# A decode step with its gradients: the scores of both halves of a chunk summed in one array tile and brought back by one-pass transposes, q and out_0 computed as rows

## The chip, the cores and the metric

One NeuronCore of one Trainium2 chip. The metric is the device time of one execution in microseconds (us). Every comparison uses runs that were rated fast, taken in alternation with the kernel before on the same chip.

## The reference, cut to what matters

A decode step of attention with 32 heads and a cache of 8192 positions, a gated MLP beside it, and the gradients of both. The gradients of the K and V caches (`out_2`, `out_3`) are as large as the caches. So all of K and V is read, and as much is written: four times 67 MB, 268 of the kernel's 303.5 MB.

```python
B, Sq, D = 1, 1, 640
Hq, Hkv, Sk, Dh = 32, 32, 8192, 128                    # bfloat16
xn = _layernorm(x)
q = (xn @ wq).reshape(B, Sq, Hq, Dh).transpose(0, 2, 1, 3)
scores = jnp.einsum("bhqd,bhkd->bhqk", q, k) * (Dh ** -0.5)
p = _softmax(scores, axis=-1)
o = jnp.einsum("bhqk,bhkd->bhqd", p, v)                # then @ wo
# + x + (silu(x @ w1) * (x @ w3)) @ w2
# reference(): the output and its vjp for x, k_cache, v_cache, wq, wo, w1, w3, w2
```

## The kernel before

For each head, K and then V (128 partitions of 64 rows of 128 bf16) go through TensorE: sixteen chunks are transposed as pairs of bf16 in fp32 words (`T`), multiplied by q or by the output gradient (`Mp`), the scores are evicted (`ev`) and brought back to one row a position by selection matmuls (`selm`). Then come softmax, the weighted sums over V and K (`wsum`), the outer products on VectorE, which overwrite K and V by their gradients, and the stores. Below are the parts that the change or the argument touches; `...` marks cuts, set-up lines of the functions are left out, and the line numbers are those of the profile.

```python
def prep_q(g, ps, first):                                # once for each group of four heads
    for hh in range(GH):
        for ci in range(NC):                             # 20 loads and matmuls of one column, L260
            nc.tensor.matmul(ps[:, hh:hh + 1], lhsT=G_["wq"][:, ci, hh * DH:(hh + 1) * DH],
                             rhs=xn_col_bf[:, ci:ci + 1], ...)
    nc.scalar.activation(G_["cb"][:, 0, :], ps, ACTF.Copy, scale=scale)

def T(h, kind, c):                                       # L305, L307
    pT = pst()
    for k in range(4):
        nc.tensor.transpose(pT[:, k * P:(k + 1) * P], W3[:, 4 * c + k, :], ident_f[:])
    KT = kt_tile()                                       # one of four buffers
    nc.scalar.copy(KT[:].rearrange("p k w -> p (k w)"), pT[:])

def Mp(h, kind, c0):                                     # QW = 32: four column groups, L324
    for c in (c0, c0 + 1):
        KTb = ...
        for par in range(2):
            q = QW * (2 * (c - c0) + par)
            o = QL + QW * (2 * a + par) - c0
            nc.tensor.matmul(S_[kind][q:q + QW, :], lhsT=S_["qz"][:, o:o + QW], rhs=KTb[:, par, :], ...)

def ev(h, kind):                                         # L330
    XS = kt_tile()
    nc.scalar.copy(XS[:].rearrange("p k w -> p (k w)"), S_.pop(kind)[:])

def selm(h, kind):                                       # L340: four fp32 matmuls, two passes each
    for k in range(4):
        nc.tensor.matmul(S_["m"][:, b0:b0 + J].rearrange("p (c k t) -> p k c t", k=4, t=2)[:, k, :, :],
                         lhsT=XS[:, k, :], rhs=selc[:].rearrange("p (c t) -> p c t", t=2), ...)

def store(kind, h):
    t = kv_tiles.pop((kind, h))
    fifo((dkc if kind == "K" else dvc)[h], t[:])
    free_slots.append(t)
    load_next()                                          # the next K or V goes into this buffer

# the end of a head's order of work
Mp(h, "V", NCH - 2)
ev(h, "V")
o_sum(h)                 # 16 matmuls of 512 columns: all that PE has during the eviction
selm(h, "V")
rdot(h)
...
# fin_pe: out_0, once for each group: 20 loads and matmuls of one column
for hh in range(GH):
    for ci in range(NC):
        nc.tensor.matmul(acc[:, OUT0 + ci:OUT0 + ci + 1], lhsT=G_["wo"][:, hh, ci * P:(ci + 1) * P],
                         rhs=G_["od_bf"][:, hh, 0:1], ...)
```

## Time and profile before

| | before |
|---|---|
| time, median of 3 runs | 732.5 us (732.12 to 733.51) |
| span of the profiled run | 730.6 us, mean granted TensorE clock 0.881 |
| TensorE busy | 606.6 us (83%), 5669 matmuls |
| DMA share, 20 to 690 us | 1.01 (424 to 428 GB/s from 100 us on) |
| PE's waits for K and V, 280 to 690 us | 30.8 us |

How to read it: a DMA share of 1.01 means that all 16 DMA engines are busy all the time. A granted clock of 0.88 means that TensorE did not run at full speed all the time. PE in a profile line is TensorE, PEld its loads of weights, DVE VectorE and ACT ScalarE; `L340` is a line of the kernel. The groups of instructions that the change touches were these (busy us, mean ns of one, idle time before and what ended it):

```profile
L340 PE MATMUL m<-selc,KT 128*128 128x16 f32 x512 | 73.2, 276 | 22.7 <-ACT KT L330 22.5
L324 PE MATMUL sA<-KT,qz 128*32 128x512 bf16 x512 | 55.1, 421 | 0.0
L330 ACT COPY KT<-dA 128x512 f32<-128x512 f32 x32 | 19.3, 604 | 0.6 <-PE dA L324 0.6
```

The selection matmuls (L340) wait 22.5 us for the eviction of the scores (L330), and each of these fp32 matmuls counts twice (x512 for 256 in the program).

### The profile page before, as it was taken

Reading aid. Unit: us, or ns where it says so; the run is one execution under the profiler, and the core shown is the slowest. Engines: PE = TensorE matmul, PEld = TensorE weight load, DVE = VectorE, ACT = ScalarE, POOL = GpSimd, SP = SyncE. Lnnn points to the kernel's source line nnn. Section 1 sums busy time; section 2 is a strip of 40 time slices with the busy share of each in tenths; the row PEclk is TensorE's granted clock in tenths of the full one; section 3 lists DMA queues with packets and bytes.
Section 4 is the critical chain, followed back from the end, with each engine's and each line's share of the span. In section 5 each row is a group of like instructions: output and inputs, shape, how many; then the busy total and the mean of one; then the engine's idle time right before and its main releaser. Section 6 shows DMA issues by size and latency. Waiting matters only on the chain.

```text
span 730.6 us, 13869 instructions
## 1 busy us (share of the span) xinstructions
PE 606.6 (83%) x5669; PEld 423.1 (58%) x5669; DVE 459.3 (63%) x806; ACT 369.4 (51%) x719; POOL 29.9 (4%) x45
## 2 busy tenths in 40 slices
PE   3989589998899889988987887888898889978940
PEld 2657466666566656666655555566566556655620
DVE  4069646677757776776646765547756756667482
ACT  2650736656556556554655554545554536655510
POOL 0010110000100000001000000000000000000000
PEclk9996699999999999988998998979897969989765
DMA  9999999999999999999999999999999999999993
GB/s 354 400 411 420 425 421 432 415 429 425 417 416 426 429 427 421 430 428 426 425 428 426 431 423 427 429 428 428 427 424 429 429 427 428 428 434 426 425 393 155
DMA packets 27145, 303.58 MB, mean 416 GB/s; under 512 B 2807, under 2 KB 4153, under 8 KB 10441
## 3 DMA queue, kind: packets, MB, share of 16 engines
q1 hardware_dynamic: 21328, 276.39, 89.5%
q0 software_dynamic: 5728, 26.30, 8.9%
q8 instruction: 44, 0.72, 0.4%
q14 instruction: 21, 0.16, 0.1%
q10 hardware_dynamic: 24, 0.01, 0.0%
HBM read 151.34 MB, written 151.34 MB: 414 GB/s over the span
## 4 chain that ended last, share of the span: by engine, by line
PE 42%; DMA 41%; DVE 8%; ACT 6%; issue 1%; SPq 0%; ACTq 0%; DVEq 0%
DMA out_dram<-kv 22%; PE pT L305 20%; DMA kv<-in_A_k_cache_dram 11%; DMA kv<-in_A_v_cache_dram 7%; PE m L340 6%; PE X L417 5%; ACT KT L307 4%; PE sA L324 4%; DVE kv L450 3%; PE dA L324 2%; DMA wo_g<-in_A_wo_dram 2%; DVE side L251 1%; PE gu_ps L527 1%; ACT KT L330 1%; PE m L430 1%
## 5 line engine op out<-in xcount | busy, mean ns | idle before, releaser
L307 ACT COPY KT<-pT 128x512 f32<-128x512 f32 x512 | 289.5, 589 | 235.3 <-PE pT L305 200.6
L305 PE MATMUL pT<-ident_f,kv 128*128 128x128 f32 x2048 | 318.7, 296 | 40.6 <-DMA kv<-in_A_k_cache_dram 17.9
L305 PEld LDWEIGHTS pT<-ident_f,kv 128*128 128x128 f32 x2048 | 248.5, 154 | 97.0 <-PE pT L305 27.8
L450 DVE TENSOR_TENSOR kv<-qd,U 128x4096 bf16<-128x4096 bf16 x64 | 146.0, 2284 | 0.0
L450 DVE TENSOR_TENSOR kv<-qd,P 128x4096 bf16<-128x4096 bf16 x64 | 143.6, 2284 | 0.0
L340 PEld LDWEIGHTS m<-selc,KT 128*128 128x128 f32 x512 | 67.4, 205 | 45.8 <-ACT KT L330 34.1
L340 PE MATMUL m<-selc,KT 128*128 128x16 f32 x512 | 73.2, 276 | 22.7 <-ACT KT L330 22.5
L417 PE MATMUL X<-kv,Z 128*32 128x512 bf16 x1024 | 85.3, 462 | 1.8 <-DVE Z L434 1.8
L400 DVE SCALAR_TENSOR_TENSOR U<-m,P 128x64 bf16<-128x64 f32 x32 | 7.4, 233 | 104.9 <-PE m L340 104.9
L324 PE MATMUL dA<-KT,qz 128*32 128x512 bf16 x512 | 55.2, 418 | 0.2 <-ACT KT L307 0.2
L324 PE MATMUL sA<-KT,qz 128*32 128x512 bf16 x512 | 55.1, 421 | 0.0
L324 PEld LDWEIGHTS <-qz 128*32 128x32 bf16 x1024 | 26.6, 93 | 42.8 <-issue 41.6
L417 PEld LDWEIGHTS <-Z 128*32 128x32 bf16 x1024 | 28.6, 110 | 33.9 <-issue 16.6
L366 DVE TENSOR_REDUCE mrow<-m 128x1 f32<-128x64 f32 x32 | 7.1, 223 | 62.9 <-PE m L340 62.9
L360 ACT CAST qd<-pT 128x256 bf16<-128x256 f32 x32 | 11.9, 372 | 48.6 <-DVE kv L450 32.4
L500 DVE SCALAR_TENSOR_TENSOR wq_g<-wq_g,side 128x512 bf16<-128x512 bf16 x40 | 27.3, 683 | 0.0
L251 DVE SCALAR_TENSOR_TENSOR side<-wo_g,g_bc 128x640 bf16<-128x640 bf16 x32 | 26.2, 819 | 1.1 <-DMA wo_g<-in_A_wo_dram 0.8
L373 DVE TENSOR_REDUCE negM<-m 128x1 f32<-128x128 f32 x32 | 9.3, 291 | 24.5 <-PE m L370 24.5
L432 DVE SCALAR_TENSOR_TENSOR U<-m,P 128x128 bf16<-128x128 f32 x32 | 11.4, 355 | 18.0 <-PE m L430 18.0
L390 DVE RECIPROCAL rZ<-m 128x1 f32<-128x1 f32 x32 | 5.3, 167 | 24.1 <-PE m L384 24.1
L330 ACT COPY KT<-dA 128x512 f32<-128x512 f32 x32 | 19.3, 604 | 0.6 <-PE dA L324 0.6
L330 ACT COPY KT<-sA 128x512 f32<-128x512 f32 x32 | 19.3, 603 | 0.0
(154 smaller groups left out, 365.2 us busy)
## 6 DMA issues: line engine op xcount, KB each, us to landing
out_dram<-kv SPq DMA_DIRECT2D x64, 2048.0 KB, 31.1
kv<-in_A_k_cache_dram SPq DMA_DIRECT2D x32, 2048.0 KB, 25.2
kv<-in_A_v_cache_dram SPq DMA_DIRECT2D x32, 2048.0 KB, 26.3
out_dram<-wo_g POOLq DMA_DIRECT2D x8, 640.0 KB, 11.4
out_dram<-wq_g POOLq DMA_DIRECT2D x8, 640.0 KB, 12.9
wq_g<-in_A_wq_dram POOLq DMA_DIRECT2D x7, 640.0 KB, 13.2
wo_g<-in_A_wo_dram POOLq DMA_DIRECT2D x7, 640.0 KB, 19.3
kv<-in_B_w_dram SPq DMA_DIRECT2D x2, 1728.0 KB, 28.7
```

The lines of the kernel that those rows point to most:

```text
L251: nc.vector.scalar_tensor_tensor(junk[:], G_["wo"][:, hh, :], 1.0, g_bc[:], ALU.mult, ALU.mult, accum_out=G_["do"][:, hh:hh + 1])
L305: nc.tensor.transpose(pT[:, k * P:(k + 1) * P], W3[:, 4 * c + k, :], ident_f[:])
L307: nc.scalar.copy(KT[:].rearrange("p k w -> p (k w)"), pT[:])
L324: nc.tensor.matmul(S_[kind][q:q + QW, :], lhsT=S_["qz"][:, o:o + QW], rhs=KTb[:, par, :], start=(c0 == 0), stop=(c0 == NCH - 2), skip_grou ...
L330: nc.scalar.copy(XS[:].rearrange("p k w -> p (k w)"), S_.pop(kind)[:])
L340: nc.tensor.matmul(S_["m"][:, b0:b0 + J].rearrange("p (c k t) -> p k c t", k=4, t=2)[:, k, :, :], lhsT=XS[:, k, :], rhs=selc[:].rearrange( ...
L360: nc.scalar.copy(qd[:].rearrange("p a d -> p (a d)"), hd[h].pop("ps_r"))
L373: nc.vector.tensor_reduce(S_["negM"][:], S_["m"][:, 2 * J:2 * J + P], AX.X, ALU.max, negate=True)
L417: nc.tensor.matmul(xg["X"][q:q + QW, :], lhsT=Z[:, o:o + QW], rhs=W[:, N4 * i:N4 * (i + 1)], start=(slot == 0 and i < 4), stop=(slot == NS ...
L432: nc.vector.scalar_tensor_tensor(S_["U2"][:], S_["V"][:, 0:J].unsqueeze(2).to_broadcast([P, J, 2]), S_["m"][:, OC + NS:OC + NS + 1], S_["P ...
L450: nc.vector.tensor_tensor(dst[:, lo * DH:hi * DH].rearrange("p (j a b) -> p j a b", a=DH // 2, b=2), vec.rearrange("p (a b) -> p a b", b=2 ...
L500: nc.vector.scalar_tensor_tensor(wq_g[:, ci, :], wq_g[:, ci, :], 1.0, dqb, ALU.mult, ALU.mult, accum_out=dxa[:, ci, g:g + 1])
```

## The change

The intent is less work on TensorE. The two halves (`par`) of a chunk are summed in the same array tile, in two rounds, so the scores take 64 partitions instead of 128. A sum of halves by the selection matrix is then no longer needed, and the way back is a permutation: a transpose, which needs one pass instead of two (the transposes of L305 count once, x2048 for 2048 in the program, the matmuls of L340 twice). q and out_0 become rows, with the weights as moving operand: few long matmuls instead of many loads of weights. The core of the diff:

```diff
+    def out_row(vec, mat):
+        k = mat.shape[0]
+        for e in range(2):
+            nc.tensor.matmul(acc[64 * e:64 * (e + 1), 0:DHALF], lhsT=vec.to_broadcast([k, 64]),
+                             rhs=mat[:, e * DHALF:(e + 1) * DHALF], start=False, stop=True, skip_group_check=True)
...
+    def prep_q(g):
+        pq = pst()
+        for ci in range(NC):
+            nc.tensor.matmul(pq[:], lhsT=xn_col_bf[:, ci:ci + 1].to_broadcast([P, P]), rhs=G_["wq"][:, ci, :], ...)
+        G_["qrow"] = t_tile()
+        nc.scalar.activation(G_["qrow"][0:1, 0:GW], pq[0:1, :], ACTF.Copy, scale=scale)
+    def prep_qc(g, ps, first):
+        for hh in range(GH):
+            nc.tensor.matmul(ps[:, hh:hh + 1], lhsT=qrow[0:1, hh * DH:(hh + 1) * DH], rhs=one_bf[0:1, :], ...)
...
     def Mp(h, kind, c0):
-            for par in range(2):
-                q = QW * (2 * (c - c0) + par)
+        for par in range(2):
+            for c in (c0, c0 + 1):
+                q = QW * (c - c0)
                 o = QL + QW * (2 * a + par) - c0
...
     def ev(h, kind):
-        nc.scalar.copy(XS[:].rearrange("p k w -> p (k w)"), S_.pop(kind)[:])
+        nc.scalar.copy(XS[0:QH].rearrange("p k w -> p (k w)"), S_.pop(kind)[0:QH, :])      # QH = 64
...
     def selm(h, kind):
         for k in range(4):
-            nc.tensor.matmul(S_["m"][:, b0:b0 + J].rearrange("p (c k t) -> p k c t", k=4, t=2)[:, k, :, :],
-                             lhsT=XS[:, k, :], rhs=selc[:].rearrange("p (c t) -> p c t", t=2),
-                             start=(kind == "K" and k == 0), stop=True, skip_group_check=True)
+            nc.tensor.matmul(S_["m"][:, b0:b0 + 4 * J].rearrange("p (x c k t) -> p k x c t", x=4, k=4, t=2)[:, k],
+                             lhsT=XS[0:QH, k, :], rhs=selc[0:QH].rearrange("p (x c t) -> p x c t", x=4, t=2),
+                             start=(kind == "K" and k == 0), stop=True, is_transpose=True, skip_group_check=True)
...
     # fin_pe, and likewise in the MLP
-            for ci in range(NC):
-                nc.tensor.matmul(acc[:, OUT0 + ci:OUT0 + ci + 1], lhsT=G_["wo"][:, hh, ci * P:(ci + 1) * P], ...)
+            out_row(G_["od_bf"][:, hh, 0:1], G_["wo"][:, hh, :])
```

Cut: small MLP tiles move into a buffer that is free by then, the sum for the gradient of x moves to another bank and is reduced earlier, x is added to out_0 by matmul, and out_0 is stored from a row, ahead of `out_1`.

More of the change, by code (lines that the diff above doesn't have):

```diff
@@ L193 @@
     RX = 64
-    dx_acc = acc[:, 0:NC * RX].rearrange("p (c r) -> p c r", r=RX)
-    OUT0 = NC * RX
+    DHALF = D // 2
+    def out_row(vec, mat):
[3 more added lines that the diff above has]
+                             rhs=mat[:, e * DHALF:(e + 1) * DHALF], start=False, stop=True, skip_group_check=True)
     negmean = consts.tile([P, 1], F32, name="negmean")
@@ L254, in prep_do @@
             nc.vector.tensor_copy(G_["cb"][:, 1, :], G_["do"][:])
-    def prep_q(g, ps, first):
+    def prep_q(g):
         G_ = grp[g]
-        for hh in range(GH):
-            for ci in range(NC):
-                nc.tensor.matmul(ps[:, hh:hh + 1], lhsT=G_["wq"][:, ci, hh * DH:(hh + 1) * DH],
-                                 rhs=xn_col_bf[:, ci:ci + 1], start=(first and hh == 0 and ci == 0),
-                                 stop=(ci == NC - 1), skip_group_check=True)
-        nc.scalar.activation(G_["cb"][:, 0, :], ps, ACTF.Copy, scale=scale)
+        pq = pst()
+        for ci in range(NC):
+            nc.tensor.matmul(pq[:], lhsT=xn_col_bf[:, ci:ci + 1].to_broadcast([P, P]), rhs=G_["wq"][:, ci, :],
+                             start=(ci == 0), stop=(ci == NC - 1))
+        G_["qrow"] = t_tile()
+        nc.scalar.activation(G_["qrow"][0:1, 0:GW], pq[0:1, :], ACTF.Copy, scale=scale)
+    def prep_qc(g, ps, first):
+        G_ = grp[g]
+        qrow = G_.pop("qrow")
+        for hh in range(GH):
+            nc.tensor.matmul(ps[:, hh:hh + 1], lhsT=qrow[0:1, hh * DH:(hh + 1) * DH], rhs=one_bf[0:1, :],
+                             start=(first and hh == 0), stop=True, skip_group_check=True)
+        nc.scalar.copy(G_["cb"][:, 0, :], ps)
     def prep_sel(g, ps):
@@ L289 @@
     Z_vals = Z[:, QW - 4:].rearrange("p (i n) -> p i n", n=QW)[:, :, 0:4]
-    selc = consts.tile([P, 2 * NCH], F32, name="selc")
-    nc.vector.tensor_tensor(
-        selc[:].rearrange("p (e o t) -> p o e t", o=2, t=2),
-        ident_f[:].rearrange("p (o b n) -> p o b n", b=2, n=QW)[:, :, 0, 0:NCH].rearrange(
-            "p o (e t) -> p o e t", t=2),
-        ident_f[:].rearrange("p (o b n) -> p o b n", b=2, n=QW)[:, :, 1, 0:NCH].rearrange(
-            "p o (e t) -> p o e t", t=2), ALU.add)
+    QH = 2 * QW
+    selc = consts.tile([P, QH], F32, name="selc")
+    for x in range(QW // NCH):
+        nc.vector.tensor_copy(
+            selc[:, 2 * NCH * x:2 * NCH * (x + 1)].rearrange("p (e o t) -> p o e t", o=2, t=2),
+            ident_f[:, 0:QH].rearrange("p (o x e t) -> p x o e t", o=2, e=NCH // 2, t=2)[:, x])
     def new_head(h):
@@ L317, in Mp @@
                 S_["V"] = ps_d.tile([P, 512], F32, name="dA", tag="dA")
+        KTb = {}
         for c in (c0, c0 + 1):
-            KTb = S_["kt"].pop((kind, c))[:].rearrange("p k w -> p (k w)").bitcast(BF16).rearrange(
+            KTb[c] = S_["kt"].pop((kind, c))[:].rearrange("p k w -> p (k w)").bitcast(BF16).rearrange(
                 "p (n two) -> p two n", two=2)
-            for par in range(2):
-                q = QW * (2 * (c - c0) + par)
+        for par in range(2):
+            for c in (c0, c0 + 1):
+                q = QW * (c - c0)
                 o = QL + QW * (2 * a + par) - c0
-                nc.tensor.matmul(S_[kind][q:q + QW, :], lhsT=S_["qz"][:, o:o + QW], rhs=KTb[:, par, :],
-                                 start=(c0 == 0), stop=(c0 == NCH - 2), skip_group_check=True)
+                nc.tensor.matmul(S_[kind][q:q + QW, :], lhsT=S_["qz"][:, o:o + QW], rhs=KTb[c][:, par, :],
+                                 start=(c0 == 0 and par == 0), stop=(c0 == NCH - 2 and par == 1),
+                                 skip_group_check=True)
     def ev(h, kind):
@@ L486, in fin_pe @@
         for hh in range(GH):
-            for ci in range(NC):
-                nc.tensor.matmul(acc[:, OUT0 + ci:OUT0 + ci + 1], lhsT=G_["wo"][:, hh, ci * P:(ci + 1) * P],
-                                 rhs=G_["od_bf"][:, hh, 0:1], start=False, stop=True, skip_group_check=True)
+            out_row(G_["od_bf"][:, hh, 0:1], G_["wo"][:, hh, :])
     def fin_wo(g):
@@ L519, with mt @@
     blocks_f = [(b, min(P, F - b * P)) for b in range(NB)]
-    hcol = consts.tile([P, NB], F32, name="hcol")
+    mt_f = mA[:, NA * F:].bitcast(F32)
+    mt_at = [0]
+    def mt(cols):
+        r = mt_f[:, mt_at[0]:mt_at[0] + cols]
+        mt_at[0] += cols
+        return r
+    hcol = mt(NB)
     def mlp():
@@ L546, in mlp @@
                                  start=False, stop=True, skip_group_check=True)
-        gu = consts.tile([P, 2, NB], F32, name="gu")
-        nc.vector.memset(gu[:], 0.0)
+        gu = mt(2 * NB).rearrange("p (w b) -> p w b", w=2)
+        nc.vector.memset(gu, 0.0)
         nc.vector.tensor_copy(gu[:, :, 0:NFULL], gu_ps[:, :, 0:NFULL])
@@ L553, in mlp @@
         up = gu[:, 1, :]
-        dhc = consts.tile([P, NB], F32, name="dhc")
-        nc.vector.tensor_reduce(dhc[:], dh_ps[:], AX.X, ALU.add)
-        sig = consts.tile([P, NB], F32, name="sig")
-        nc.scalar.activation(sig[:], gate, ACTF.Tanh, scale=0.5)
-        nc.vector.tensor_scalar(sig[:], sig[:], 0.5, 0.5, ALU.mult, ALU.add)
-        silu = consts.tile([P, NB], F32, name="silu")
-        nc.vector.tensor_tensor(silu[:], gate, sig[:], ALU.mult)
-        nc.vector.tensor_tensor(hcol[:], silu[:], up, ALU.mult)
@@ L562, in mlp @@
-        hcol_bf = consts.tile([P, NB], BF16, name="hcol_bf")
-        nc.vector.tensor_copy(hcol_bf[:], hcol[:])
-        dgu = consts.tile([P, 2, NB], F32, name="dgu")
-        nc.vector.tensor_tensor(dgu[:, 1, :], dhc[:], silu[:], ALU.mult)
-        t1 = consts.tile([P, NB], F32, name="t1")
-        nc.vector.tensor_scalar(t1[:], sig[:], -1.0, 1.0, ALU.mult, ALU.add)
-        nc.vector.tensor_tensor(t1[:], t1[:], gate, ALU.mult)
-        nc.vector.tensor_scalar(t1[:], t1[:], 1.0, None, ALU.add)
@@ L570, in mlp @@
-        nc.vector.tensor_tensor(t1[:], t1[:], sig[:], ALU.mult)
-        nc.vector.tensor_tensor(dgu[:, 0, :], dhc[:], up, ALU.mult)
-        nc.vector.tensor_tensor(dgu[:, 0, :], dgu[:, 0, :], t1[:], ALU.mult)
-        dgu_bf = consts.tile([P, 2, NB], BF16, name="dgu_bf")
-        nc.vector.tensor_copy(dgu_bf[:], dgu[:])
+        dhc = mt(NB)
+        nc.vector.tensor_reduce(dhc, dh_ps[:], AX.X, ALU.add)
+        sig = mt(NB)
+        nc.scalar.activation(sig, gate, ACTF.Tanh, scale=0.5)
+        nc.vector.tensor_scalar(sig, sig, 0.5, 0.5, ALU.mult, ALU.add)
@@ new lines, in mlp @@
+        silu = mt(NB)
+        nc.vector.tensor_tensor(silu, gate, sig, ALU.mult)
+        nc.vector.tensor_tensor(hcol, silu, up, ALU.mult)
+        hcol_bf = mt(NB // 2).bitcast(BF16)
+        nc.vector.tensor_copy(hcol_bf, hcol)
+        dgu = mt(2 * NB).rearrange("p (w b) -> p w b", w=2)
+        nc.vector.tensor_tensor(dgu[:, 1, :], dhc, silu, ALU.mult)
+        t1 = mt(NB)
+        nc.vector.tensor_scalar(t1, sig, -1.0, 1.0, ALU.mult, ALU.add)
+        nc.vector.tensor_tensor(t1, t1, gate, ALU.mult)
@@ L575, in mlp @@
+        nc.vector.tensor_scalar(t1, t1, 1.0, None, ALU.add)
+        nc.vector.tensor_tensor(t1, t1, sig, ALU.mult)
+        nc.vector.tensor_tensor(dgu[:, 0, :], dhc, up, ALU.mult)
+        nc.vector.tensor_tensor(dgu[:, 0, :], dgu[:, 0, :], t1, ALU.mult)
+        dgu_bf = mt(NB).bitcast(BF16).rearrange("p (w b) -> p w b", w=2)
+        nc.vector.tensor_copy(dgu_bf, dgu)
         for b, rows in blocks_f:
             wsrc = w2a[:, b, :] if b < NBA else w2b[:, b - NBA, :]
-            for ci in range(NC):
-                nc.tensor.matmul(acc[:, OUT0 + ci:OUT0 + ci + 1], lhsT=wsrc[0:rows, ci * P:(ci + 1) * P],
-                                 rhs=hcol_bf[0:rows, b:b + 1], start=False, stop=True, skip_group_check=True)
+            out_row(hcol_bf[0:rows, b:b + 1], wsrc[0:rows, :])
@@ new lines, in mlp @@
+        x_cb = mt(4).bitcast(BF16)[:, 0:NC]
+        nc.vector.tensor_copy(x_cb, x_col[:])
+        for ci in range(NC):
+            for e in range(2):
+                lo, hi = max(ci * P, e * DHALF), min((ci + 1) * P, (e + 1) * DHALF)
+                if lo < hi:
+                    nc.tensor.matmul(acc[64 * e:64 * (e + 1), lo - e * DHALF:hi - e * DHALF],
+                                     lhsT=x_cb[:, ci:ci + 1].to_broadcast([P, 64]),
+                                     rhs=ident_bf[:, lo - ci * P:hi - ci * P], start=False, stop=True,
+                                     skip_group_check=True)
@@ L605, in mlp @@
                 nc.scalar.copy(bc_sb[:, wi, f0:f1], pb[:, 0:f1 - f0])
+        dx_acc = ps_d.tile([P, NC, RX], F32, name="dx_acc", tag="dA")
+        nc.vector.memset(dx_acc[:], 0.0)
         FA, FB = 256, 832
@@ L633, in mlp @@
         load_next()
+        nc.vector.tensor_reduce(dxm[:], dx_acc[:], AX.X, ALU.add)
+    dxm = consts.tile([P, NC], F32, name="dxm")
     gate = consts.tile([P, 1], F32, name="gate")
@@ L674, in side_pe1, with side_pe1b @@
         elif hh == 3 and g + 1 < NG:
-            prep_q(g + 1, hd[h]["m"][:, 320:320 + GH], False)
+            prep_q(g + 1)
+    def side_pe1b(h):
+        g, hh = divmod(h, GH)
+        if hh == 3 and g + 1 < NG:
+            prep_qc(g + 1, hd[h]["m"][:, 320:320 + GH], False)
     def side_pe2(h):
@@ L732, in head @@
         T(h, "V", 7)
+        side_pe1b(h)
         Mp(h, "V", 4)
@@ L762 @@
     ps_0 = pst()
-    prep_q(0, ps_0[:, 0:GH], True)
+    prep_q(0)
+    prep_qc(0, ps_0[:, 0:GH], True)
     for hh in range(GH):
@@ L786 @@
         fin_wq(NG - 1, ci)
-    fin = consts.tile([P, 2 * NC], F32, name="fin")
-    dxm = consts.tile([P, NC], F32, name="dxm")
-    nc.vector.tensor_reduce(dxm[:], dx_acc, AX.X, ALU.add)
+    fin = consts.tile([P, NC], F32, name="fin")
     dxn = consts.tile([P, NC], F32, name="dxn")
@@ L793 @@
     nc.vector.tensor_tensor(dxn[:], dxn[:], dxm[:], ALU.add)
-    nc.vector.tensor_tensor(fin[:, 0:NC], acc[:, OUT0:OUT0 + NC], x_col[:], ALU.add)
+    row_bf = t_tile()[:, 0:DHALF]
+    nc.vector.tensor_copy(row_bf, acc[:, 0:DHALF])
+    out_0v = out_0.rearrange("a b (e c) -> (a b e) c", e=2)
+    for e in range(2):
+        nc.scalar.dma_start(out_0v[e:e + 1, :], row_bf[64 * e:64 * e + 1, :])
     st = consts.tile([P, 2], F32, name="st")
@@ L805 @@
     nc.vector.tensor_scalar(t5[:], t5[:], nst[:, 0:1], rstd[:], ALU.add, ALU.mult)
-    nc.vector.tensor_tensor(fin[:, NC:2 * NC], t5[:], g_col[:], ALU.add)
+    nc.vector.tensor_tensor(fin[:], t5[:], g_col[:], ALU.add)
     ps_o = pst()
-    nc.tensor.transpose(ps_o[0:2 * NC, 0:P], fin[:], ident_f[:])
-    fin_bf = consts.tile([2 * NC, P], BF16, name="fin_bf")
-    nc.vector.tensor_copy(fin_bf[:], ps_o[0:2 * NC, 0:P])
-    for dst, r0, cuts in ((out_0, 0, (0, 3, 5)), (out_1, NC, (0, 4, 5))):
-        for lo, hi in zip(cuts, cuts[1:]):
-            nc.scalar.dma_start(dst.rearrange("a b (c p) -> (a b c) p", p=P)[lo:hi, :], fin_bf[r0 + lo:r0 + hi, :])
+    nc.tensor.transpose(ps_o[0:NC, 0:P], fin[:], ident_f[:])
+    fin_bf = consts.tile([NC, P], BF16, name="fin_bf")
+    nc.vector.tensor_copy(fin_bf[:], ps_o[0:NC, 0:P])
+    nc.scalar.dma_start(out_1.rearrange("a b (c p) -> (a b c) p", p=P), fin_bf[:])
 _INS = ['A_x', 'A_k_cache', 'A_v_cache', 'A_wq', 'A_wo', 'B_x', 'B_w1', 'B_w3', 'B_w2', 'grad_out']
```

## The prediction

> **What bounds the kernel now.** I began with the page: 730.6 us of span, PE 83% busy, DVE 63%, ACT 51%. That looks like a TensorE kernel, so the second thing read was the row of 40 slices, which says something else.
>
> ```profile
> PE   3989589998899889988987887888898889978940
> ...
> DMA  9999999999999999999999999999999999999993
> GB/s 354 400 411 420 425 421 432 415 429 425 417 416 426 429 427 421 430 428 426 425 428 426 431 423 427 429 428 428 427 424 429 429 427 428 428 434 426 425 393 155
> DMA packets 27145, 303.58 MB, mean 416 GB/s; under 512 B 2807, under 2 KB 4153, under 8 KB 10441
> ```
>
> The 16 DMA engines show 9 tenths or more in every slice but the last, at 415 to 434 GB/s from the fourth slice to the 38th. The 303.58 MB at 428 GB/s are 709 us by themselves; start and end make the rest of 731. To see where each stage is limited I cut the span into stages (columns: PE, PEld, DVE, ACT and POOL busy us, granted clock, DMA share, GB/s):
>
> ```profile
> 20.00:100.00 80.00, 62.58 (x670) 45.44 (x669) 51.27 (x100) 34.42 (x48) 7.45 (x13) 0.80 1.01 414
> 100.00:280.00 180.00, 165.52 (x1626) 115.99 (x1624) 121.02 (x204) 108.73 (x221) 7.06 (x9) 0.97 1.01 424
> 280.00:690.00 410.00, 358.09 (x3199) 246.98 (x3198) 257.99 (x418) 214.33 (x428) 13.05 (x16) 0.88 1.01 428
> 690.00:704.00 14.00, 10.74 (x94) 7.09 (x93) 9.46 (x13) 4.93 (x11) 0.00 (x0) 0.83 0.89 377
> ```
>
> From 20 to 690 us the DMA share is 1.01. The list of PE's waits in the same stages tells which engine leads. Between 100 and 280 us PE never waits for a transfer: computing is behind, because the MLP at head 2 held it up. From 280 us on PE waits for the arrival of K and V:
>
> ```profile
> PE pT L305 <- DMA kv<-in_A_k_cache_dram: 17.9, 10, 3.8
> PE pT L305 <- DMA kv<-in_A_v_cache_dram: 12.9, 7, 2.6
> ```
>
> (us in total, times, longest.) The pace of both stages comes from the starts of the K score return (line 340) in the chain of waits. Head 3 is at 123.93 and head 10 at 251.24 us: 18.19 us a head where TensorE leads. Head 11 is at 270.56 and head 31 at 690.05: 20.97 us a head where the transfers lead. So TensorE has 2.78 us a head to spare, and it needed about ten heads to catch up.
>
> Last, the end. From 720 us no engine computes, and the DMA share of seven one-microsecond windows from 722 to 729 us averages 0.064, which is one engine of 16:
>
> ```profile
> 724.00:725.00 1.00, 0.00 (x0) 0.00 (x0) 0.00 (x0) 0.00 (x0) 0.00 (x0) 0.50 0.09 37
> 725.00:726.00 1.00, 0.00 (x0) 0.00 (x0) 0.00 (x0) 0.00 (x0) 0.00 (x0) 0.50 0.05 20
> ```
>
> The last instructions wait as follows:
>
> ```profile
> SPq L839 <- DMA out_dram<-fin_bf: 11.6, 1, 11.6
> SPq L839 <- DMA out_dram<-wq_g: 9.4, 1, 9.4
> SPq L839 <- DMA out_dram<-kv: 0.4, 1, 0.4
> ```
>
> The small outputs (fin_bf) are done 9.8 us before the big stores of wq_g and kv have landed. One DMA engine still works off its share of these while the 15 others are finished. The last kv store is issued at 707.5 us and lands near 730, 22 us later. At 428/16 = 26.8 GB/s one engine's share of it (131 KB) is 4.9 us and of the two weight stores 3.1 us[...]. So about 12 us of that time are backlog from earlier stores. My reading: the slowest DMA engine was never empty, and the time is its total work.
>
> [...] four score matmuls of 512 columns take 0.41 us together, and 16 of the weighted sums, four rounds of four, 1.03 us, so a round more is 0.21 us. [...]
>
> **The change part by part**, at full clock.
>
> (1) Score matmuls. Before, both parities of two chunks lay in four column groups of 32: one round of four. Now the parities of a chunk meet in the same group, so two rounds of two. The rows for the four:
>
> ```profile
> 268.94 0.42 PE L324 MATMUL sA<-KT,qz 128*32 128x512 bf16 x4
> 269.29 1.09 PE L305 MATMUL pT<-ident_f,kv 128*128 128x128 f32 x8
> 270.56 1.07 PE L340 MATMUL m<-selc,KT 128*128 128x16 f32 x8 [0.18 <-ACT KT L330]
> ```
>
> One round more is 0.21 us; eight such groups a head: +1.70 us.
>
> (2) The way back (line 340). Today four fp32 matmuls run as eight passes: weight loads 0.97 us for the eight. As transposes they are four passes, as in line 305, whose eight loads take 0.86 us: 0.43 us for four. Saving 0.54 us, twice a head: -1.08 us. The eviction of the score tile keeps its 512 columns (0.60 us), only on 64 partitions; I expect no gain there.
>
> (3) q as a row, once for each group of four heads. Before: 20 loads and matmuls of one column. The trace shows 20 of the same kind (line 488) starting at 375.22, with the next work at 375.72: 0.50 us. Now five matmuls of 512 columns at 0.21 us (1.07) and four one-row loads (0.1): about +0.7 us. Besides, ACT evicts a row of 512 (0.59 us by the row of line 307, against 0.17 for the old 4-column eviction). The row also takes one of the four KT buffers, so the eviction of the seventh V chunk has to wait until the chunk before is used; the scale copy queues behind it. I estimate up to 1 us of PE standing still. Sum about +1.7 us a group, +0.4 us a head.
>
> (4) out_0 as a row: 20 loads (0.50 us) become eight matmuls of 320 columns in two column groups, four rounds of 320/512 x 0.21 = 0.13: 0.53 us. Nothing. In the MLP 70 loads become 28 matmuls in 14 rounds, 1.75 us before and 1.87 after. The sum tile of dx moves to another bank, its memset and reduction (0.49 us each) with it, inside the MLP where computing is hidden.
>
> (5) The end: a row copy of 320 columns instead of the small add and the late dx reduction; three small stores instead of four, two issued earlier. The small outputs were already 9.8 us ahead of the end: nothing.
>
> Sum: +1.70 - 1.08 + 0.4 = about +1.0 us a head of TensorE's own pace, 18.2 to 19.2, which stays under 20.97. The 26.3 us by which head 2 is late (108.23 against 690.05 - 29 x 20.97 = 81.9) are then caught up at 1.8 us a head, about head 17 instead of 11, long before head 31. Break-even is 26.3/29 = 0.9 us of headroom, an increase of 1.87 us a head. In the last two heads, which TensorE leads (no DMA wait after 654.6), the final stores come 2 us later; they join a queue that is 12 us deep on the slow engine. The bytes are the same but for instruction fetch: 256 + 88 + 96 + 42 - 6 = 476 pairs fewer, some 950 of 13869 instructions. I estimate this, by the 0.88 MB of the two instruction queues, at 0.06 MB: 0.1 us if spread over the engines, 2 us at most if all of it lay on the late one.
>
> So PE busy time changes by some +10 to +30 us and the total by about 0: 732.5 becomes 732.
>
> **The rivals.** *Rival A: TensorE becomes the bound.* For it: 83% busy, and the score rounds double. Against: the 2.78 us a head to spare, and PE's 30.8 us of waiting for transfers, which soak up work first. If the increase were 3 us a head instead of 1[...], the end would come (3 - 1.87) x 29 = 33 us later: about 765 us. At 2.2 us it would be 10 us, part of it hidden by the backlog: 735 to 742.
> *Rival B: the shorter way back pays.* DVE waits 104.9 us for the V scores' return, PE stands still before it, and the chain gives line 340 5.9%. If TensorE's latency set the pace, 64 returns x 0.54 = 35 us would be won: 698 us. Against: no stage has free DMA time for it; it would need 303.58 MB in 698 us, 435 GB/s from first to last, while start and end run below 400.
> *Rival C: the tail.* If the final small stores set the end, the shorter finish would win 1 us; the waits above say they don't. If the slow engine does run dry in the last heads, 2 us are lost: 734.
>
> **Range and chances.** The floor is the transfers, which the change leaves alone, and the three runs before lie within 1.4 us. I take 728.5 to 737: below for fewer instruction fetches, above for starved transfers in the catching-up stage (single windows there already drop to 401 GB/s) and the end. Faster by over 2% would be under 717.9, beyond what the middle rate allows: 0.02. Slower by over 2% is over 747, which needs 2.4 us a head or more: 0.04. Within: 0.94.
>
> **What would show it.** Right: score groups of four at about 0.62 us, returns with four passes at about 0.43 us of loads, DMA at 425 to 430 GB/s in the middle, first PE waits for K or V later than 281 us (around 350 to 450), fewer of them than 30.8 us, and an end where one DMA engine works alone. Wrong: DMA shares below 0.95 in the middle, no PE waits for transfers at all, K score returns of late heads more than 21.3 us apart, or a late DMA engine that no longer exists at the end.

The forecast's sum came to +1.70 - 1.08 + 0.4 = about +1.0 us a head and 732 us in all. Why (2) counts passes and not rows was measured only afterwards (0.96 us for eight loads of 64 rows, 0.97 for eight of 128). Another was a term of the 22 us from the issue of the last store to its landing: by the terms that are left the "about 12 us" of backlog and the queue "12 us deep" are 14 us (22 - 4.9 - 3.1).

## The result and the profile after

| | before | after |
|---|---|---|
| median, same rounds (6 runs each) | 732.96 us (731.86 to 733.97) | 732.42 us (731.55 to 733.64) |
| profiled span, granted clock | 730.6 us, 0.881 | 731.1 us, 0.923 |
| instructions | 13869 | 12909 |
| PE busy | 606.6 us | 602.7 us |
| PE's waits for K and V, 280 to 690 us | 30.8 us | 57.9 us |

The ratio after/before is 0.9995, with a 95% interval of 0.9981 to 1.0008: the same. A ratio here is the mean time of one kernel's fast runs over that of the other's fast runs of the same rounds, so it is not quite the ratio of the medians quoted.

The page of the kernel after, to be held against the four lines that the prediction opens with:

```profile
PE 602.7 (82%) x5193; PEld 376.1 (51%) x5193; DVE 461.3 (63%) x811; ACT 375.8 (51%) x727; POOL 29.9 (4%) x45
...
GB/s 344 403 410 422 424 429 426 418 421 424 422 407 428 428 425 424 425 428 431 423 430 425 431 424 428 427 430 426 426 428 427 430 425 429 429 429 430 430 407 130
DMA packets 27135, 303.53 MB, mean 415 GB/s; under 512 B 2798, under 2 KB 4146, under 8 KB 10434
```

The same bytes at the same rate. The stages of the kernel after (PE, PEld, DVE, ACT, POOL busy us, clock, DMA share, GB/s):

```profile
100.00:280.00 180.00, 172.05 (x1523) 107.32 (x1522) 123.95 (x209) 112.65 (x227) 6.77 (x9) 0.98 1.01 422
280.00:690.00 410.00, 347.02 (x2909) 213.45 (x2909) 256.04 (x415) 216.64 (x431) 13.05 (x16) 0.94 1.01 428
```

From 280 to 690 us PE is busy 347.0 instead of 358.1 us, the clock is 0.94 instead of 0.88, and the DMA share is still 1.01. What TensorE gained, part of it by the higher clock, went into waiting. PE's longest waits there in the kernel after:

```profile
PE pT L318 <- DMA kv<-in_A_v_cache_dram: 29.5, 15, 3.0
PE pT L318 <- DMA kv<-in_A_k_cache_dram: 28.4, 15, 3.0
```

That is 57.9 us against 30.8. PE's first wait for a load ends at 302.8 us (head 13). In the kernel before the first such wait ends at about 355 us (head 16).

The groups that answer to the three of before, in the kernel after:

```profile
L339 PE MATMUL sA<-KT,qz 128*32 128x512 bf16 x512 | 83.9, 408 | 0.0
L356 PE MATMUL m<-selc,KT 64*128 64x64 f32 x256 | 30.2, 240 | 8.1 <-ACT KT L346 7.9
L346 ACT COPY KT<-dA 64x512 f32<-64x512 f32 x32 | 18.6, 583 | 3.1 <-PE dA L339 3.1
```

The scores cost 57 us more (K and V together 110.3 to 167.7), the way back 43 us less (73.2 to 30.2). The eviction of half the partitions is hardly shorter (604 to 583 ns). The timeline of the kernel after shows single groups at full clock (start us, duration us):

```profile
325.93 0.32 PEld L356 LDWEIGHTS m<-selc,KT 64*128 64x128 f32 x4 [0.17 <-issue]
325.94 0.46 PE L356 MATMUL m<-selc,KT 64*128 64x64 f32 x4
326.32 0.12 PEld L339 LDWEIGHTS <-qz 128*32 128x32 bf16 x4
326.32 0.63 PE L339 MATMUL dA<-KT,qz 128*32 128x512 bf16 x4
```

A score group takes 0.63 us (0.42 before), and a way back 0.32 us of loads (0.97 before). The end is as it was. The last waits of the kernel after:

```profile
SPq L880 <- DMA out_dram<-wq_g: 12.0, 1, 12.0
SPq L880 <- DMA out_dram<-KT: 9.1, 1, 9.1
...
SPq L880 <- DMA out_dram<-kv: 2.2, 1, 2.2
```

The rows of out_0 (KT) have landed at 715.7 us, long before the big stores (727.7 and 730.1). From 722 to 730 us the DMA share is 0.06, one engine of 16, as before.

### The profile page after: what moved, and what is told of

Its sections match the earlier page's. It is cut to its first block, busy times and chain, and to the rows that moved or that the text cites. A ratio compares the mean times of both kernels' runs of the same rounds, so it can differ in the third digit from the quotient of the medians.

```text
span 731.1 us, 12909 instructions
## 1 busy us (share of the span) xinstructions
PE 602.7 (82%) x5193; PEld 376.1 (51%) x5193; DVE 461.3 (63%) x811; ACT 375.8 (51%) x727; POOL 29.9 (4%) x45
## 2 busy tenths in 40 slices
DMA packets 27135, 303.53 MB, mean 415 GB/s; under 512 B 2798, under 2 KB 4146, under 8 KB 10434
## 4 chain that ended last, share of the span: by engine, by line
DMA 51%; PE 35%; DVE 6%; ACT 3%; issue 1%; SPq 0%; ACTq 0%; DVEq 0%
DMA kv<-in_A_k_cache_dram 22%; DMA out_dram<-kv 17%; PE pT L318 16%; DMA kv<-in_A_v_cache_dram 11%; PE sA L339 4%; PE dA L339 3%; PE X L433 3%; DVE kv L466 3%; PE m L356 2%; DMA wo_g<-in_A_wo_dram 2%; ACT KT L320 1%; ACT kv L630 1%; PE gu_ps L549 1%; PE dh_ps L560 1%; PE dx_acc L648 1%
## 5 line engine op out<-in xcount | busy, mean ns | idle before, releaser
L318 PE MATMUL pT<-ident_f,kv 128*128 128x128 f32 x2048 | 308.2, 290 | 60.3 <-DMA kv<-in_A_v_cache_dram 29.5
L318 PEld LDWEIGHTS pT<-ident_f,kv 128*128 128x128 f32 x2048 | 237.1, 149 | 153.7 <-issue 52.2
L433 PE MATMUL X<-kv,Z 128*32 128x512 bf16 x1024 | 94.3, 405 | 1.8 <-DVE Z L450 1.8
L339 PE MATMUL sA<-KT,qz 128*32 128x512 bf16 x512 | 83.9, 408 | 0.0
L339 PE MATMUL dA<-KT,qz 128*32 128x512 bf16 x512 | 83.8, 406 | 0.0
L433 PEld LDWEIGHTS <-Z 128*32 128x32 bf16 x1024 | 32.5, 99 | 34.5 <-issue 6.9
L356 PE MATMUL m<-selc,KT 64*128 64x64 f32 x256 | 30.2, 240 | 8.1 <-ACT KT L346 7.9
L356 PEld LDWEIGHTS m<-selc,KT 64*128 64x128 f32 x256 | 21.3, 142 | 30.1 <-ACT KT L346 21.2
L389 DVE TENSOR_REDUCE negM<-m 128x1 f32<-128x128 f32 x32 | 9.3, 292 | 33.3 <-PE m L386 33.3
L346 ACT COPY KT<-dA 64x512 f32<-64x512 f32 x32 | 18.6, 583 | 3.1 <-PE dA L339 3.1
L346 ACT COPY KT<-sA 64x512 f32<-64x512 f32 x32 | 18.6, 580 | 2.3 <-PE sA L339 1.9
```

The costliest lines, as they stand in the source:

```text
L346: nc.scalar.copy(XS[0:QH].rearrange("p k w -> p (k w)"), S_.pop(kind)[0:QH, :])
L356: nc.tensor.matmul(S_["m"][:, b0:b0 + 4 * J].rearrange("p (x c k t) -> p k x c t", x=4, k=4, t=2)[:, k], lhsT=XS[0:QH, k, :], rhs=selc[0:Q ...
L389: nc.vector.tensor_reduce(S_["negM"][:], S_["m"][:, 2 * J:2 * J + P], AX.X, ALU.max, negate=True)
L433: nc.tensor.matmul(xg["X"][q:q + QW, :], lhsT=Z[:, o:o + QW], rhs=W[:, N4 * i:N4 * (i + 1)], start=(slot == 0 and i < 4), stop=(slot == NS ...
```

## The experiments

Two questions stay open after the result. Is the time the same because transfers bind, or because TensorE's cost did not change? And what does each part of the change cost on TensorE? My theory was that transfers bind; the rival was that TensorE's gains and losses cancel. For the first question extra work is put on TensorE or bytes are taken away. For the second, stores are cut to a quarter (202.9 instead of 303.5 MB), which takes the transfers off the path so that TensorE's cost shows in the time (the DMA share from 280 to 600 us is 0.80 in q4_before and 0.85 in q4_after, and in neither is one of PE's nine largest waits for K or V). A kernel with cut stores leaves three quarters of `out_2` and `out_3` unwritten; its other outputs are right unless said otherwise. "Before" is the full kernel before on the same chip: 733.65, 733.66 and 732.76 us on the three chips used.

| run | median us (lowest to highest) | ratio to full before, 95% | clock of the profiled run |
|---|---|---|---|
| q4_before | fast runs 693.79 and 693.66; two more, slow, 707.87 and 705.6 | none given | 0.893 |
| q4_after | 652.98 (647.53 to 655.04) | 0.889 [0.8848, 0.8931] | 0.957 |
| q4_after_twopass | 709.14 (707.33 to 710.6) | 0.9666 [0.9643, 0.9689] | 0.935 |
| q4_after_fourgroups | 630.69 (627.92 to 633.72) | 0.8599 [0.8567, 0.863] | 0.935 |
| q4_after_oldq | 656.17 (652.77 to 659.16) | 0.8945 [0.8907, 0.8983] | 0.949 |
| full_T4 | 736.0 (734.76 to 737.16) | 1.0029 [1.0002, 1.0056] | 0.949 |
| full_T8 | 757.6 (756.79 to 757.76) | 1.0327 [1.0307, 1.0347] | 0.969 |
| full_hw | 741.42 (740.19 to 743.01) | 1.011 [1.0083, 1.0137] | 0.92 |
| full_before_T4 | 734.17 (733.66 to 735.57) | 1.0013 [0.9993, 1.0033] | 0.923 |
| full_before_T8 | 762.34 (760.43 to 768.12) | 1.0408 [1.0362, 1.0453] | 0.94 |
| q4_before_filled | 661.48 (661.02 to 661.82) | 0.9019 [0.9002, 0.9035] | 0.946 |
| full_after_s78 | 693.88 (693.24 to 694.74) | 0.9458 [0.9437, 0.9478] | 0.939 |

### Stores cut to a quarter, before and after

```diff
-        fifo((dkc if kind == "K" else dvc)[h], t[:])
+        fifo((dkc if kind == "K" else dvc)[h][:, 0:KVN // 4], t[:, 0:KVN // 4])
```

> The kernel before, with a quarter of the columns of dK and dV stored (wrong outputs on purpose), which takes 100.7 MB of stores away: about 5.9 MB a head, 13.8 us at 428 GB/s, less than TensorE's 18.2 us a head. Theory D (the transfers set the time of the full kernel): the time falls until TensorE's pace sets it, 732.5 - 29 heads x 2.78 = about 652 us, range 630 to 672, and PE stops waiting for K and V loads after the first heads. Rival (TensorE or the tail sets the time already): it stays within 2% of 732.

> The changed kernel with the same cut of the stores. By the pace read from the two profiles where TensorE leads (heads 3 to 10: 18.19 us a head before, 17.90 after) it is 29 x 0.29 = 8 us faster than the kernel before with the same cut (theory: the added score rounds are mostly hidden in waits that the V side has anyway). By the sum of my prediction (+1.0 us a head) it is 29 us slower. By the rival of the shorter way back it is some 35 us faster.

Measured: 693.7 us in the two fast runs before, 652.98 us after. Both expectations missed; nearest is the rival's "some 35 us faster", but the sections below show that most of the 41 us is granted clock and not shorter instructions. The kernel before is over 40 us slower than expected although TensorE sets its time, and the change is worth about 41 us here, where my working gave a loss of some 29. The two slow runs of q4_before (clock 0.876 and 0.878, against 0.893) are used for nothing; whether the chip or the kernel made them slow is open, and with two fast runs the difference has no interval. It is far larger than the spread of any other run.

What follows: with the stores cut, TensorE's pace did change, by a lot, and for the better. In the full kernels something else hides it; that this is the bytes is shown further down, by the run with 7/8 of the stores and those with added work. How much of the 41 us the full kernels have too is a question of its own: where the clock is full, the two kernels differ by only 0.2 us a head, so the rival's "gains and losses cancel" is nearly right there.

### Parts of the change, with stores cut

Two passes again, from the 64-partition tile:

```diff
-                             lhsT=XS[0:QH, k, :], rhs=selc[0:QH].rearrange("p (x c t) -> p x c t", x=4, t=2),
-                             start=(kind == "K" and k == 0), stop=True, is_transpose=True, skip_group_check=True)
+                             lhsT=XS[0:QH, k, :], rhs=selc[0:QH, 0:2 * NCH].rearrange("p (c t) -> p c t", t=2),
+                             start=(kind == "K" and k == 0), stop=True, skip_group_check=True)
```

> The changed kernel, stores cut, with the way back as ordinary two-pass fp32 matmuls again (from the 64-partition tile, so the score rounds stay doubled). If each pass saved is on TensorE's path, two returns a head x about 0.5 us x 29 to 32 heads make it 29 to 35 us slower than the changed kernel with the same cut. If the V return is hidden, about half: 15 us. If neither counts: within 5 us.

Four column groups again, with the one-pass way back of the lower 64 partitions (half of each score is lost, so gradients are wrong; the work on each engine is what counts; the start and stop flags of the matmul change with it):

```diff
-                q = QW * (c - c0)
+                q = QW * (2 * (c - c0) + par)
```

> The changed kernel, stores cut, with the score matmuls in four column groups as before, and the one-pass return of the lower 64 partitions only (so half of each score is lost: wrong on purpose). If the second round of all eight groups a head is on the path: 8 x 0.21 x 29 to 32 = 49 to 54 us faster than the changed kernel with the same cut. If only the K side's four count and the V side's are hidden in waits: about 25 us faster. If none counts: within 5 us.

The old q for groups 1 to 7:

```diff
-            prep_q(g + 1)
+            prep_q_old(g + 1, hd[h]["m"][:, 320:320 + GH], False)      # the 20 one-column matmuls
```

> The changed kernel, stores cut, with q made by the old 20 loads of one column for groups 1 to 7 (group 0 keeps the row). My prediction put the row at +1.7 us a group: 7 groups make this 12 us faster than the changed kernel with the same cut. If the standing still that I estimated does not happen, only the 0.7 us of matmul time counts: 5 us faster. If it is hidden: within 3 us.

Measured, against q4_after's 652.98: two passes +56 us, beyond the largest case expected; four groups -22 us, near the case in which only the K side counts; old q +3 us with overlapping intervals and on another chip. The mean pace (start of the K scores' way back in head 31 less that in head 3, over 28) gives a square of two parts, in us a head:

| | two passes back | one pass back | saved by one pass |
|---|---|---|---|
| four score groups | 19.19 (q4_before) | 17.13 (fourgroups) | 2.06 |
| two score groups | 19.58 (twopass) | 17.81 (q4_after) | 1.77 |
| cost of the second round | 0.39 | 0.68 | |

In the first head of a group of four, where it runs at full clock, the four corners are 17.4, 16.1, 18.4 and 17.2 (in the order q4_before, fourgroups, twopass, q4_after). There, one pass saves 1.2 us a head, about what the loads say: (0.97 - 0.32) x 2 = 1.30. The second round costs 1.1 us, less than the 1.70 worked out. The second head of a group takes 16.6 us in fourgroups and the same as the first in the others, so there the corner of fourgroups gives 0.7 for the pass and 0.6 for the round: the parts do not simply add. The V side's eviction is waited for, and scores that end later shorten that wait: in first and second heads at full clock it is 1.08 and 1.80 us in q4_before, 0.32 and 1.33 in twopass. These 0.5 to 0.8 us are about the 0.6 us by which the round costs less than worked out; no run isolates it.

The row for q costs hardly anything: the interval of the head that makes q is 18.7 us with the row and 18.3 with the old q, 0.4 us a group where I had 1.7.

Were rows or passes what the shorter way back comes from? The loads of the two-pass kernel with 64 partitions and of q4_after, in that order (PE's weight loads, start and duration in us):

```profile
448.01 0.96 PEld L356 LDWEIGHTS m<-selc,KT 64*128 64x128 f32 x8 [0.42 <-ACT KT L346]
```

```profile
455.63 0.32 PEld L356 LDWEIGHTS m<-selc,KT 64*128 64x128 f32 x4 [1.83 <-ACT KT L346]
```

Eight loads of 64 rows take 0.96 us, as eight of 128 rows did (0.97). Halving the partitions shortened nothing. Half the passes did, and a pass of the transpose is also shorter (0.08 us against 0.12).

### Where the rest of the 41 us comes from: the wait before the V scores' way back

The full-clock heads differ by only 0.2 us (17.4 and 17.2), but the means by 1.38 us. So most of the gain is in heads that are not at full clock. PE's waits for the eviction of the scores, in q4_before and then in q4_after (total us, times, longest):

```profile
PE m L340 <- ACT KT L330: 41.7, 31, 2.0
```

```profile
PE m L356 <- ACT KT L346: 23.4, 22, 1.6
```

and what happens around one of them in q4_before, in the timeline of PE (start, duration, in brackets the wait):

```profile
547.07 1.03 PE L417 MATMUL X<-kv,Z 128*32 128x512 bf16 x16
549.90 1.51 PE L340 MATMUL m<-selc,KT 128*128 128x16 f32 x8 [1.80 <-ACT KT L330]
...
553.86 1.92 PE L417 MATMUL X<-kv,Z 128*32 128x512 bf16 x16
```

Sixteen matmuls of the same line and shape (L417) take 1.03 us before the wait of 1.80 us and 1.92 us four us after its end. The granted clock (the third number from the right) in windows of q4_before says why:

```profile
547.00:550.00 3.00, 1.20 (x21) 0.41 (x13) 1.96 (x5) 1.84 (x4) 0.00 (x0) 1.00 1.01 431
550.00:553.00 3.00, 3.00 (x17) 3.00 (x18) 0.60 (x4) 0.56 (x1) 0.00 (x0) 0.56 0.05 16
553.00:556.00 3.00, 3.00 (x25) 1.01 (x24) 3.00 (x3) 0.61 (x2) 0.00 (x0) 0.50 0.00 0
```

To test whether the wait costs clock, 14 small matmuls that nobody needs were put into it, in the kernel before with cut stores. All other work stayed as it was:

```diff
         o_sum(h)
+        for _ in range(14):
+            nc.tensor.matmul(hd[h]["m"][:, 2 * J:2 * J + P], lhsT=ident_bf[:], rhs=ident_bf[:],
+                             start=False, stop=True, skip_group_check=True)
         selm(h, "V")
```

> The kernel before, stores cut to a quarter (699.7 us; its clock 0.89 from 280 to 600 us, against 0.99 for the changed kernel), with 14 useless bf16 matmuls of 128 columns a head put where TensorE waits for the eviction of the V scores (31 waits of 1.3 us). Theory (that wait makes the granted clock fall to half for a stretch in most heads, which costs some 1.5 to 2 us a head): filling it keeps the clock up, near 0.98, and the time falls by 20 to 45 us although TensorE does more. Rival (the clock is not what differs): the time stays, or grows by up to 14 x 0.06 x 32 = 27 us.

Measured: 661.48 us, 32 us less than q4_before's fast runs, with more work (the two ran on different chips, whose full kernels before differ by 0.9 us). The stretch from 280 to 600 us of q4_before, then of the filled kernel, then of q4_after:

```profile
280.00:600.00 320.00, 294.58 (x2700) 206.40 (x2689) 218.22 (x351) 178.03 (x362) 11.45 (x14) 0.89 0.80 297
```

```profile
280.00:600.00 320.00, 307.68 (x3207) 219.01 (x3206) 236.64 (x389) 195.11 (x397) 12.19 (x15) 0.99 0.85 319
```

```profile
280.00:600.00 320.00, 303.29 (x2710) 189.19 (x2714) 236.76 (x391) 198.16 (x400) 12.22 (x15) 0.99 0.85 314
```

The clock goes from 0.89 to 0.99 by filling alone, as it does with the change. In heads at full clock both kernels take the same time (17.37 us in the first of a group), so the added matmuls cost nothing there; what changes is that 5 of the 28 heads from 3 to 30 lose clock instead of 17. So most of the change's gain on TensorE in this regime can be had without any shorter instruction: 32 of the 41 us. That the clock is lost after many such waits (17 heads), and mostly kept when they are filled (lost in 5), is shown. That the change keeps it by shorter waits (23.4 against 41.7 us) is not, and other traces speak against length alone: twopass has the same waits as q4_after (23.4 us, 22 times, up to 1.6) and loses clock in 13 heads where q4_after does in 3, fourgroups keeps a clock of 0.97 (280 to 600 us) with 33.3 us of waits of up to 2.0, and heads 4, 5 and 6 of q4_before have waits of 1.08, 1.80 and 2.00 us at full clock. What decides it is open.

### How much TensorE work is hidden

4 or 8 of the 16 transposing steps of a head are done twice (results are right):

```diff
-        for k in range(4):
+        for k in [0, 1, 2, 3] * (2 if (kind, c) in [('K', 4), ('K', 5), ('V', 2), ('V', 6)] else 1):   # T4
```

> The changed kernel with all its stores, in which four of the 16 transposing steps a head are issued twice (same result): 4 x 0.43 = 1.7 us of TensorE more a head. Theory D (the transfers set the time, TensorE has 20.97 - 17.90 = 3.1 us a head to spare and about 2.2 before the end moves): within 1% of 732. Rival (TensorE's path counts): 29 x 1.7 = 50 us slower.

> Eight of 16 transposing steps twice: 3.4 us of TensorE more a head, over the spare time. Theory D: now TensorE sets the end, (3.4 - 2.2) x 29 = 37 us later, some of it hidden: 750 to 770 us. If the time stays at 732, the spare time is larger than I read it.

> The kernel before, all stores, four of 16 transposing steps a head issued twice (+1.7 us of TensorE a head). The changed kernel with this load took 736.0 us. Theory: the change bought TensorE about 1.4 us a head (19.19 to 17.81 us a head between heads 3 and 31 with the stores cut), which is room the transfers hide; so the kernel before, with the same load, has 19.19 + 1.7 = 20.9 us a head and no room left: 745 to 765 us. Rival (no room was bought, the full kernels have the same spare time): 733 to 738, as the changed one.

> The kernel before, all stores, eight of 16 steps twice (+3.4 us a head). The changed kernel with this load took 757.6. Theory: 29 x 1.4 = 40 us more than that, less what the full clock gives back[...]: 775 to 800. Rival (no room bought): 757.

Measured on the kernel after: 736.0 and 757.6 us, as expected. With four steps more PE still waits for K and V from 280 to 690 us, 19.7 us in all:

```profile
PE pT L318 <- DMA kv<-in_A_k_cache_dram: 10.3, 9, 2.4
PE pT L318 <- DMA kv<-in_A_v_cache_dram: 9.4, 7, 2.1
```

With eight it never does, and the transfers run dry before the end (T8, the same columns as above):

```profile
704.00:720.00 16.00, 14.69 (x140) 10.12 (x140) 10.22 (x17) 7.54 (x16) 0.86 (x1) 1.00 0.51 207
```

The mean pace of T8 from head 3 to head 31 is 20.98 us. The prediction put break-even at 18.19 + 1.87 = 20.06 us a head, so an estimate from its formula is (20.98 - 20.06) x 29 = 27 us later; measured are 25.

On the kernel before I was wrong: with four steps 734.17 us where I expected a clear loss, and with eight 762.34, below what I expected. So the room that the change buys is not the 41 us that the cut stores suggest. It is about 5 us with eight steps (the two ran on different chips, whose full kernels before differ by 0.9 us), and nothing can be seen with four. Even these 5 us are clock and not shorter work: in heads at full clock the kernel before is the faster one with eight steps (20.36 us a head against 20.61, first of a group), but 9 of its 28 heads lose clock and none of the kernel after. In both kernels before with extra work the clock is high (0.95 and 0.97 in their middle stage), although with eight steps PE waits for the eviction nearly as long in all as in q4_before (41.7 us there):

```profile
PE m L340 <- ACT KT L330: 40.0, 29, 1.8
```

Why the clock is lost so much less there is open.

### Fewer bytes, and another queue

7/8 of the columns of dK and dV are stored, in the kernel after:

```diff
-        fifo((dkc if kind == "K" else dvc)[h], t[:])
+        w_ = KVN * 7 // 8
+        fifo((dkc if kind == "K" else dvc)[h][:, 0:w_], t[:, 0:w_])
```

> The changed kernel with 7 of 8 columns of dK and dV stored (wrong on purpose): 16.8 MB fewer of 303.5. Theory (transfers set the time, byte for byte): 16.8 MB at 428 GB/s = 39 us less, 693 us, as TensorE's 17.9 us a head stays below the transfers' 21.0 - 1.2 = 19.8. Rival (the end or TensorE sets it): 720 or more.

Measured: 693.88 us, as expected, with these bytes:

```profile
DMA packets 27135, 286.75 MB, mean 414 GB/s; under 512 B 2798, under 2 KB 4146, under 8 KB 10434
```

16.8 MB less take 38.5 us less, a slope of 435 GB/s, and one DMA engine is again alone at the end (share 0.07 to 0.04 from 686 to 692 us). The time follows the bytes.

All transfers of the GpSimd queue issued by SyncE instead, with the loads of a group two heads later:

```diff
-        nc.gpsimd.dma_start(dwq_v[:, :, g * GW:(g + 1) * GW], wq_g[:])
+        nc.sync.dma_start(dwq_v[:, :, g * GW:(g + 1) * GW], wq_g[:])        # and the others likewise
```

> The changed kernel with every transfer that GpSimd issued (weights in and out, MLP gradients) issued by SP instead, loads of a group two heads later. It asks where the single DMA engine that finishes 9 us after the others comes from. [...] If it is slow for another reason, the lone stretch stays and so does the time, 730 to 736; if SP waits too long in its order, it grows.

The case cut there is that the engine is late because of the GpSimd queue; the last 8 us, with one engine at work, would then go, down to about 725 us. It was a guess that no trace had shown.

Measured: 741.42 us, 1.1% slower. The number of packets rises from 27135 to 40878 and the middle rate falls to 414 GB/s. At the end several engines are late instead of one (DMA share 0.40, 0.29, 0.17, 0.06 from 732 to 740 us in steps of 2). The experiment changed packet sizes as well as the queue, so it does not tell why one engine is late.

## Why the prediction was right, and which of its steps were wrong

- **The bound: right, and shown.** The time follows bytes (seven eighths of the stores: -38.5 us), and four transposing steps a head (1.7 us, at 0.43 us of loads each) can be added for 0.3% (T4). A kernel that is 41 us faster when stores are cut is not faster with them. The number does not confirm the sum over a head: by the prediction's own formula, anything below +1.87 us a head would have been hidden.
- **The reading of the stages: partly wrong.** "From 280 us on PE waits for the arrival of K and V": the first such wait of the kernel before ends at 355 us. Its heads 12 to 14 are slow (18.9 to 20.6 us) without one, at a granted clock of 0.83 to 0.91. So part of the pace of 20.97 us, and of the 2.78 us a head taken as spare, was clock.
- **Score groups: the duration right, the sum over a head too large.** 0.63 us measured, 0.62 predicted. "+1.70" a head shows as 1.1 at full clock, in some heads 0.6.
- **The way back: too small.** "0.43 us for four" was taken from transposes of 128 rows and 128 moving columns. Measured are 0.32 us, so the step is -1.30 a head and not -1.08. The eviction was as expected (604 to 583 ns, no gain worth the name).
- **The q row: too large.** "About +1.7 us a group" is 0.4. The "up to 1 us of PE standing still" did not show.
- **out_0 and the end: right.** No cost seen. Last compute ends at 717.2 us (718.4 before), and the end is set by a late DMA engine as before. The backlog of "about 12 us" does not follow from the terms in the text: 22 - 4.9 - 3.1 is 14 us.
- **The sum: the wrong step.** "About +1.0 us a head" should have been about -0.15 at full clock: 1.06 - 1.30 + 0.1 by the parts measured above, and 17.37 to 17.22 in the trace. By the prediction's own measure, the pace from head 3 to head 10, 18.19 became 17.90 us and not 19.2. From this followed the wrong signs. PE busy was to grow by 10 to 30 us and fell by 3.9 (at a clock of 0.923 instead of 0.881, which shortens it by itself: sixteen matmuls of L417 took 1.03 us at a clock of 1.00 and 1.92 at 0.50); the waits for loads were to be fewer than 30.8 us and nearly doubled; the first was to come at 350 to 450 us and came at 302.8. What was right is that a change of this size on TensorE is hidden.
- **The missing term: the granted clock.** I worked at full clock and gave the 0.88 of the middle stage no place in the sum. With transfers off the path the kernel before still lost clock after its wait for the V scores (1.00 up to the end of the wait of 1.80 us shown, then 0.56 and 0.50), and filling that wait raised the clock from 0.89 to 0.99 and gave 32 us.
- **Rival B had the mechanism, not the effect.** "The shorter way back pays" is true on TensorE: 2.06 and 1.77 us a head with stores cut, 0.7 to 1.2 of it at full clock. It fell, as the prediction said, because no stage has free DMA time for it (a DMA share of 1.01 from 100 to 690 us in both kernels).

No run beats both full kernels with right results.

## What to carry to other kernels

The DMA share was 1.01 from 100 to 690 us here, and what TensorE gained turned into waiting for loads (30.8 to 57.9 us); in a kernel with such a profile, look for a gain in those waits. Cutting the stores to a quarter brought it into the time, but at another clock (0.99 in the kernel after instead of 0.94, 280 to 600 us) and much too large: 41 us, against about 5 us or nothing in the full kernels with added work. So add work to the full kernels as well. Sum instruction durations for a part, but check the sum by swapping one part at a time: here the second round cost 1.1 us instead of 1.70, and the mean pace of the two kernels differed by 1.38 us a head where heads at full clock differ by 0.2. A loss of clock after a wait can cost more than the wait: with the waits of up to 2.0 us filled, 12 more of the 28 heads kept the clock and 32 us were won, by estimate 2.7 us for each of them (32/12), though in heads 4, 5 and 6 of q4_before waits of 1.08 to 2.00 us cost no clock. A test with useless small matmuls told so in one run.
